# Four weight-sum columns beside the experts, expert inputs in two single buffers, and the norm's vector in the weights

## Chip, cores and metric

One core of a Trainium2 chip runs the whole program. The metric is the device time of one execution in microseconds, the median over the runs shown. TensorE multiplies, VectorE, ScalarE and GpSimd do the elementwise work, and DMAs are issued from the queue of SP (SyncE) and, for gathers, from GpSimd's.

## The reference, cut to what matters

Three layers follow each other: a windowed attention, a layer of eight experts of which each token uses two, and a gated layer behind a root-mean-square norm. The change touches the last two.

```python
x = attention(q, k, v)                         # 2304 tokens x 512
top2 of (x @ w_gate + noise * log1p(exp(x @ w_noise)))
out[t] = sum over the token's 2 experts e of weight * (relu(x[t] @ w1[e]) @ w2[e])   # 512 -> 1024 -> 512
x = out
rms = sqrt(mean(x * x) + 1e-6)
xn = x / rms * rms_g
g, val = xn @ w_gate, xn @ w_val               # 512 -> 1536 each
y = (g * sigmoid(g) * val) @ w_out             # 1536 -> 512
```

## The kernel before, in words

**Numbers as pairs.** Matrices are kept as two float16 parts, a rounded high part and the rest; a product takes three matmuls (high by high, low by high, high by low). ScalarE rounds (the high part), VectorE or GpSimd subtracts (the low part).

**Experts.** Each expert has room for 640 tokens (`CAP`). `row_steps` (lines 169 to 176) brings its rows from memory turned, by five DMA transposes, into the tile `xT`, of which there are two (experts take turns between two pools, `epool`). `expert_steps` (222) works in two pieces, 384 and 256 tokens: `first_steps` (178) makes hidden units in eight slices, with ScalarE's `hh` (194) and VectorE's `hl` (195) after each, then `second_steps` (206) multiplies them back. While expert e runs, VectorE and ScalarE also split the weights of expert e+1 (`weight_steps`, 98), and `m2_steps` (653) decodes and splits six slices of the gated layer's weights, scaled by a constant (662 to 666): the gate's in experts 1 and 2, the value's in 3 and 4, the output's in 5 and 6.

**The gated layer.** The first two tiles of 128 tokens go plainly: `gated` (858) makes gate and value products (line 880) for 12 chunks of 128 columns, and `projected` (903) multiplies with the output weights (914). The other 16 tiles go in four blocks of four through `quads` (1040), which needs 7 products in place of 8 per pair of chunks: sums of weight blocks times sums of token blocks (987). There are 12 such weight columns (6 chunk pairs by gate and value). For each, `weight_sums` (927) has VectorE make 8 sums (938), ScalarE round 4 (941) and GpSimd subtract 4 (944). Three columns are made beside the last expert (`SOON`), nine beside the first tiles of the gated layer. Their places are in `xpool`, `hpool` and `ppool`.

**Tokens of the gated layer.** `combine` (797) gathers each token's two expert rows by GpSimd (763), mixes them on VectorE (769, 770), normalizes by the root and the vector `rms_g` (`normal`, 745, with the vector broadcast to all partitions in `gb`), makes the token sums (823 to 826), splits them (837, 838) and turns them by DMA transposes into the one buffer `xq` (843). `combine_first` (773) does the first two tiles beside the last expert.

**Order.** Each engine runs its instructions in the order in which the program issues them, and the program writes this order by hand. `drive` (146) counts columns that TensorE has been given, and whenever a side task's due point (start, pace, task) is reached it issues that task's next step. One column count of 256 is one matmul of 256 columns. So `(0, SUMS, weight_sums(...))` with `SUMS` = 3200 issues one fifth of a weight column each 3,200 columns. The due points of the two main calls are at 1064 and 1094; those of the experts at 704 and 709. Pools that close return their room, and a tile put there waits for the last use of the tile that lay in its place.

Of the kernel before, what the change touches and what calls it, by code (L numbers as in the profile page):

```python
# [13 lines left out]
F32 = mybir.dt.float32  # L14
# [18 lines left out]
SOON, SUM0, SUMS = 3, 6000, 3200  # L33
# [8 lines left out]
def attention_moe_swiglu(  # L42
# [34 lines left out]
    hpool = ctx.enter_context(tc.tile_pool(name="hpool", bufs=1))  # L77
    early = ctx.enter_context(ExitStack())
# [16 lines left out]
    gb = consts.tile([P, DM], F32, name="gb")  # L95
# [73 lines left out]
    def row_steps(e, cs, taken=None):  # L169
        if cs.start == 0:  # L170
            xts[e] = epool[e % 2].tile([P, 2 * KC, CAP], F16, name="xT")
        for c in range(cs.start, cs.stop, P):
            ins = nc.sync.dma_start_transpose(xts[e][:, :, c:c + P], xrows[e * N + c:e * N + c + P, :])
            if taken is not None:
                taken.append(ins)
            yield

    def first_steps(hp_, w1h, w1l, xT, *pieces):
# [3 lines left out]
        for cs, f in itertools.product(pieces, range(FC)):  # L182
# [4 lines left out]
            for w1, xo in ((w1h, 0), (w1l, 0), (w1h, KC)):  # L187
                for c in range(KC):
                    nc.tensor.matmul(hp[:, :w], w1[:, c, f * P:(f + 1) * P], xT[:, xo + c, cs],  # L189
# [32 lines left out]
    def expert_steps(e, *pieces):  # L222
        w1h, w1l, w2h, w2l = wts[e]
        steps = first_steps(hpool, w1h, w1l, xts[e], *pieces)
# [14 lines left out]
    with ExitStack() as actx:  # L239
# [171 lines left out]
        def constants():  # L411
# [15 lines left out]
            nc.vector.tensor_scalar(gb, gb, SN, None, op0=OP.mult)  # L427
# [35 lines left out]
        def route(t0, nb):  # L463
# [49 lines left out]
            if t0 < 10:  # L513
# [9 lines left out]
        nc.sync.dma_start(gb, bass.AP(tensor=moe2_rms_g.tensor, offset=moe2_rms_g.offset,  # L523
                                      ap=[[0, P], [1, DM]]))
# [112 lines left out]
    m2w = ctx.enter_context(tc.tile_pool(name="m2w", bufs=1, side="right", reuse_waits="tile"))  # L637
    epool.append(late.enter_context(tc.tile_pool(name="epool1", bufs=1, side="right", reuse_waits="tile")))
    dec = late.enter_context(tc.tile_pool(name="dec", bufs=1, side="right", reuse_waits="tile"))
# [56 lines left out]

    coming = {}

    def ahead(e):
        if e < E:  # L700
# [5 lines left out]
          *((50000 + 9000 * i, 500, row_steps(1, cs)) for i, cs in enumerate(HALVES)),  # L706
          (40000, 4000, mix()), (70000, 5000, ahead(2)))
    for e in range(1, E - 1):
        drive(itertools.chain(*(expert_steps(e, cs) for cs in HALVES)),
              (2000, 3000, coming.pop(e + 1)), (106000, 5000, ahead(e + 2)),  # L710
              *((46000 + 17000 * i, 2000, row_steps(e + 1, cs)) for i, cs in enumerate(HALVES)),
              (48000, 2900, m2_steps([m2_part(i) for i in range(6 * (e - 1), 6 * e)])))

    early.close()
# [5 lines left out]
    HQ, QW, FH = QT // 2, QT // 2 * P, GC // 2  # L720
# [15 lines left out]
    def inverse(mp, vv, r):  # L736
# [36 lines left out]
    def combine_first(mp, xnT):  # L773
# [7 lines left out]
        for n in range(2 * FIRST + 3):  # L781
            for i in range(FIRST):
# [9 lines left out]
                elif j == 4:  # L792
                    inverse(mp, *rs[i])
                    turned(mp, x3s[i], rs[i][1], columns(xnT, i), nc.vector if i == FIRST - 1 else nc.gpsimd)
            yield

    def combine(mp, t0, xq):
# [19 lines left out]
        for j, (a, b) in enumerate(pairs):  # L817
            xa, xb = x3s[a], x3s[b]
            tt = mp.tile([P, 3, K2], F32, name="tt", bufs=1)
            normal(xa, r[:, a:a + 1])  # L820
            normal(xb, r[:, b:b + 1])
# [7 lines left out]
            for x in (xa, xb, tt[:, :2].rearrange("p k d -> p (k d)"), tt[:, 2]):  # L829
# [3 lines left out]
                else:  # L833
                    xn = mp.tile([P, DM], F16, name="xh", bufs=1)
# [11 lines left out]
    def normalize(mp, x3s, xnT):  # L846
# [5 lines left out]
        for i, x3 in enumerate(x3s):  # L852
            turned(mp, x3, r[:, i:i + 1], columns(xnT, i), nc.gpsimd)
# [68 lines left out]

    def weight_sums(mp, sw, chunks):
        for i, m in chunks:
            blocks = {}
            for a, k in itertools.product(range(2), range(2)):  # L930
                cs = slice((a * FH + i) * P, (a * FH + i + 1) * P)
# [235 lines left out]
```

## Time and profile before

| | us |
|---|---|
| median of 3 runs | 984.01 (982.09 to 984.03) |
| the profiled execution | 982.35 |
| its span, first to last instruction | 980.6 |
| TensorE busy | 950.8 (97%) |
| VectorE busy | 652.7 (67%) |
| ScalarE busy | 450.3 (46%) |
| GpSimd busy | 212.9 (22%) |

Attention runs until about 150 us, the experts until 564.6, the first two tiles of the gated layer until 623.3, and the four blocks of four tiles until the end. The clock granted to TensorE reads 9 (90% or more) in each of the page's 40 slices.

How to read it: PE is TensorE, PEld its weight loads, DVE VectorE, ACT ScalarE, POOL GpSimd, SPq the DMA queue of SP. "out<-in" names tiles, L938 a line of the kernel. In a bracket stands the idle time before an instruction and what ended it.

### The profile page before, as it was taken

What the parts mean: (1) busy time and instruction counts of PE and PEld (TensorE: products, weight loads), DVE (VectorE), ACT (ScalarE), POOL (GpSimd) and SP (SyncE); (2) the same over time, 40 slices, a digit from 0 to 9 for tenths busy, and PEclk for the clock granted to TensorE, in tenths of its full rate; (3) what the DMA queues carried; (4) which work ended last, traced back from release to release, by engine and by line L of the source; (5) the groups of instructions that cost most, each with busy time, mean ns of one, the idle gap of its engine ahead of it and who ended that gap; (6) DMA issues with size and microseconds to landing.
All of it is one profiled execution on the core that took longest, in us unless ns stands there. A gap on an engine that the chain in (4) does not pass through costs nothing.

```text
span 980.6 us, 18518 instructions
## 1 busy us (share of the span) xinstructions
PE 950.8 (97%) x7220; PEld 663.9 (68%) x7220; DVE 652.7 (67%) x1503; ACT 450.3 (46%) x920; POOL 212.9 (22%) x255
## 2 busy tenths in 40 slices
PE   7999999999999999999999997989999999999997
PEld 5998896656565555656565684678478658847864
DVE  6788767357576766666665579999458817944850
ACT  7999865254544444454533344434223422522320
POOL 5567644000000000000002364631601230130000
PEclk9999999999999999999999999999999999999999
DMA  7989667757584948495740242211431160122000
GB/s 235 309 246 241 176 184 200 208 158 208 174 234 151 250 137 220 156 230 168 210 112 14 76 114 44 60 54 33 105 69 33 22 151 1 34 64 57 1 13 35
DMA packets 145279, 127.12 MB, mean 130 GB/s; under 512 B 97696, under 2 KB 114848, under 8 KB 145184
## 3 DMA queue, kind: packets, MB, share of 16 engines
q1 hardware_dynamic: 139424, 106.99, 40.8%
q0 software_dynamic: 5760, 18.88, 5.8%
q8 instruction: 58, 0.95, 0.4%
q14 instruction: 37, 0.30, 0.1%
HBM read 76.81 MB, written 26.74 MB: 106 GB/s over the span
## 4 chain that ended last, share of the span: by engine, by line
PE 87%; DVE 7%; DMA 2%; ACT 1%; issue 1%; POOL 1%; SPq 1%; DVEq 0%; ACTq 0%; POOLq 0%
PE acc L210 21%; PE mm L189 21%; PE mm L987 21%; PE acc L914 11%; PE acc L363 6%; PE mm L349 4%; DVE sums L938 3%; PE mm L321 3%; DMA xq<-xg 1%; SPq L843 1%; DVE pgl L896 1%; PE rt L460 0%; PE mm L880 0%; DVE ya L770 0%; DMA yb<-ybuf,ysl 0%
## 5 line engine op out<-in xcount | busy, mean ns | idle before, releaser
L189 PE MATMUL mm<-xT,w1h 128*128 128x256 f16 (+2 forms) x1088 | 164.8, 291 | 0.0
L195 DVE SCALAR_TENSOR_TENSOR hl<-mm,hh 128x256 f16<-128x256 f32 (+2 forms) x136 | 63.8, 469 | 104.3 <-ACT hh L194 104.1
L189 PEld LDWEIGHTS <-w1h 128*128 128x128 f16 x1088 | 103.9, 98 | 37.8
L210 PE MATMUL acc<-w2h,hh 128*128 128x512 f16 x320 | 121.3, 379 | 0.0
L210 PE MATMUL acc<-w2l,hh 128*128 128x512 f16 x320 | 121.3, 379 | 0.0
L210 PE MATMUL acc<-w2h,hl 128*128 128x512 f16 x320 | 121.3, 379 | 0.0
L944 POOL TENSOR_TENSOR sw<-sums,sw 128x256 f16<-128x256 f32 x36 | 28.5, 810 | 387.9 <-ACT sw L941 387.9
L210 PEld LDWEIGHTS <-hh 128*128 128x128 f16 x640 | 62.6, 98 | 72.8
L987 PE MATMUL mm<-xq,sw 128*128 128x256 f16 x864 | 100.5, 273 | 1.6 <-DMA xq<-xg 1.5
L194 ACT ACTIVATE hh<-mm 128x256 f16<-128x256 f32 (+2 forms) x136 | 56.8, 418 | 85.8 <-PE mm L189 83.6
L987 PEld LDWEIGHTS <-sw 128*128 128x128 f16 x864 | 84.3, 98 | 12.3 <-issue 1.8
L189 PE MATMUL mm<-xT,w1l 128*128 128x256 f16 (+2 forms) x544 | 92.2, 291 | 0.0
L914 PE MATMUL acc<-oh__3213,pgl 128*128 128x512 f16 (+2 forms) x228 | 84.0, 371 | 2.9 <-DVE pgl L896 2.9
L914 PE MATMUL acc<-oh__3213,pgh 128*128 128x512 f16 (+2 forms) x228 | 83.9, 370 | 0.4 <-ACT pgh L894 0.4
L914 PE MATMUL acc<-ol__3214,pgh 128*128 128x512 f16 (+2 forms) x228 | 84.0, 371 | 0.0
L914 PEld LDWEIGHTS <-pgh 128*128 128x128 f16 x456 | 44.3, 99 | 49.9 <-issue 1.4
L363 PE MATMUL acc<-v,pf 128*128 128x96 f32 x544 | 72.6, 276 | 0.0
L363 PEld LDWEIGHTS acc<-v,pf 128*128 128x128 f32 x544 | 68.5, 197 | 0.0
L332 DVE CUSTOM_DVE_ANT_0 ss<-mm,bias 128x256 f32<-128x256 f32 (+1 forms) x144 | 54.1, 398 | 17.3 <-PE mm L321 11.5
L341 ACT ACTIVATE pr<-ss,nm 128x256 f32<-128x256 f32 (+1 forms) x144 | 63.2, 490 | 3.7 <-DVE nm L332 3.4
L189 PEld LDWEIGHTS <-w1l 128*128 128x128 f16 x544 | 52.1, 98 | 17.7
L232 ACT ACTIVATE ys<-acc 128x512 f32<-128x512 f32 x40 | 23.7, 593 | 77.3 <-PE acc L210 68.9
(190 smaller groups left out, 1721.0 us busy)
## 6 DMA issues: line engine op xcount, KB each, us to landing
st<-in_moe_w SPq DMA_DIRECT2D x64, 512.0 KB, 4.4
ybuf<-ys SPq DMA_DIRECT2D x40, 256.0 KB, 2.5
raw<-in_qkv SPq DMA_DIRECT2D x17, 512.0 KB, 5.3
st<-in_moe_w_gate SPq DMA_DIRECT2D x12, 512.0 KB, 5.0
st<-in_moe_w_val SPq DMA_DIRECT2D x12, 512.0 KB, 4.8
st<-in_moe_w_out SPq DMA_DIRECT2D x12, 512.0 KB, 5.2
v<-in_qkv SPq DMA_DIRECT2D x18, 279.0 KB, 5.3
out<-ys SPq DMA_DIRECT2D x17, 256.0 KB, 2.2
```

Source lines behind the costliest of these rows:

```text
L189: nc.tensor.matmul(hp[:, :w], w1[:, c, f * P:(f + 1) * P], xT[:, xo + c, cs], start=(n == 0), stop=(n == 3 * KC - 1))
L194: nc.scalar.activation(hh[:, f, hs], hp[:, :w], AF.Relu)
L195: nc.vector.scalar_tensor_tensor(hl[:, f, hs], hp[:, :w], 0.0, hh[:, f, hs], op0=OP.max, op1=OP.subtract)
L210: nc.tensor.matmul(yp, hx[:, f, i * P:(i + 1) * P], w2[:, f, :], start=(n == 0), stop=(n == 3 * FC - 1))
L321: nc.tensor.matmul(st[n + i]["sp"][:, j, c:c + w * P], qT[t][ds, a, h // 2, :], kT[ds, b, h // 2, sl:sl + w, :], start=(m == 0), stop=(m = ...
L332: nc.vector.tensor_tensor_reduce(out=d["ss"][:, j, c0:], in0=d["sp"][:, j, c0:], in1=bias[kind][:, heads(d["hp"])[j], c0:], scale=-1.0 / K ...
L341: nc.scalar.activation(d["pr"][:, j, c0:], d["ss"][:, j, c0:], AF.Exp, scale=-1.0, bias=d["nm"][:, j:j + 1])
L349: nc.tensor.transpose(pt[:, j, kk, :], d["pr"][:, j, kk * P:(kk + 1) * P], ident)
L363: nc.tensor.matmul(xps[t, hp // 2][:, h % 4, :VN], ph[:, j, kk, :], v32[t - 1 + kk][:, h * DV:h * DV + VN], start=(kk == k0), stop=(kk == 1))
L914: nc.tensor.matmul(op[:, ds], px[:, f, cs], w[:, f, ds], start=(k == 0), stop=(k == 3 * GC - 1))
L938: nc.vector.tensor_tensor(out=o, in0=x, in1=y, op=op)
L987: nc.tensor.matmul(pp, w(a, pa, c), xq[:, 4 * b + 2 * pb + c, :], start=(n == 0), stop=(n == 5))
```

## The change

- Four of the nine weight columns that were made beside the gated layer are made beside experts 3 to 6, one in each (30,000 columns into the expert, a step each 5,500), in a new pool `spool`. Three are still made beside the last expert, at a pace of 3,000 columns per step in place of 6,000, and five beside the gated layer, at 4,400 in place of 3,200. They use fewer temporary buffers: one in `spool` and one in `mp`, by turns.
- The expert inputs lie in two tiles, `xA` (384 tokens) and `xB` (256), one of each, in place of two `xT`. The second piece of an expert's rows is now brought at that expert's own start (due at 1,000 columns), no longer in the expert before.
- The vector of the norm is multiplied into gate and value weights where they are split: `gain` holds it by rows of the weights (with the constants), and `m2_part` hands a column of it as scale. `normal` goes; tokens are scaled by the root alone, on ScalarE (`combine`, `turned`). `SN` moves into the last step of `inverse`.
- Buffers of the gated layer (`gt`, `vt`, `p1`, `tt`, `xh`) move to a pool `mp2` on the other side; some sums' places move into `xA` and `xB`; the pool `dec` closes earlier.

```diff
-SOON, SUM0, SUMS = 3, 6000, 3200
+SOON, SUM0, SUMS = 3, 3000, 4400
...
     def row_steps(e, cs, taken=None):
-        if cs.start == 0:
-            xts[e] = epool[e % 2].tile([P, 2 * KC, CAP], F16, name="xT")
+        first = cs.start < GW
+        if cs.start in (0, GW):
+            xts[e, first] = xpiece.tile([P, 2 * KC, GW if first else CAP - GW], F16, name="xA" if first else "xB")
...
-        nc.sync.dma_start(gb, bass.AP(tensor=moe2_rms_g.tensor, offset=moe2_rms_g.offset,
-                                      ap=[[0, P], [1, DM]]))
+        nc.sync.dma_start(gain[:, 0], moe2_rms_g.rearrange("(c p) -> p c", p=P))
...
-            src, sc = ((moe2_w_gate, SWG), (moe2_w_val, SWV))[m]
-            return (src[c * P:(c + 1) * P, n0:n0 + DM], sc, *(x[:, c, n0:n0 + DM] for x in gw[2 * m:2 * m + 2]))
+            src = (moe2_w_gate, moe2_w_val)[m]
+            return (src[c * P:(c + 1) * P, n0:n0 + DM], gain[:, m, c:c + 1], *(x[:, c, n0:n0 + DM] for x in gw[2 * m:2 * m + 2]))
...
+    chunks = list(itertools.product(range(FH), range(2)))
+    EARLIER = {3: [(0, 0)], 4: [(1, 0)], 5: [(0, 1)], 6: [(1, 1)]}
+    BESIDE = len(EARLIER)
+    sw = {at: [spool.tile([P, 2, 2, 2, P], F16, name=f"sw{at[0]}{at[1]}_{j}") for j in range(2)] for at in chunks[:BESIDE]}
...
-          *((50000 + 9000 * i, 500, row_steps(1, cs)) for i, cs in enumerate(HALVES)),
+          (50000, 500, row_steps(1, HALVES[0])),
           (40000, 4000, mix()), (70000, 5000, ahead(2)))
     for e in range(1, E - 1):
         drive(itertools.chain(*(expert_steps(e, cs) for cs in HALVES)),
               (2000, 3000, coming.pop(e + 1)), (106000, 5000, ahead(e + 2)),
-              *((46000 + 17000 * i, 2000, row_steps(e + 1, cs)) for i, cs in enumerate(HALVES)),
+              (1000, 2000, row_steps(e, HALVES[1])), (46000, 2000, row_steps(e + 1, HALVES[0])),
+              (30000, 5500, weight_sums([spool], sw, EARLIER.get(e, ()))),
               (48000, 2900, m2_steps([m2_part(i) for i in range(6 * (e - 1), 6 * e)])))
...
-        nc.vector.tensor_tensor(out=r, in0=r, in1=u, op=OP.mult)
-    def normal(x3, r):
-        nc.vector.scalar_tensor_tensor(x3, x3, r, gb, op0=OP.mult, op1=OP.mult)
-    def turned(mp, x3, r, xnT, lo):
-        normal(x3, r)
+        nc.vector.scalar_tensor_tensor(r, r, SN, u, op0=OP.mult, op1=OP.mult)
+    def turned(mp, x3, r, xnT):
         xn = mp.tile([P, 2 * DM], F16, name="xg", bufs=3)
-        nc.vector.tensor_copy(xn[:, :DM], x3)
-        lo.tensor_tensor(out=xn[:, DM:], in0=x3, in1=xn[:, :DM], op=OP.subtract)
+        nc.scalar.activation(xn[:, :DM], x3, AF.Copy, scale=r)
+        nc.vector.scalar_tensor_tensor(xn[:, DM:], x3, r, xn[:, :DM], op0=OP.mult, op1=OP.subtract)
...
-            normal(xa, r[:, a:a + 1])
-            normal(xb, r[:, b:b + 1])
+            for i in (a, b):
+                nc.scalar.activation(x3s[i], x3s[i], AF.Copy, scale=r[:, i:i + 1])
...
-        drive(itertools.chain(*(expert_steps(E - 1, cs) for cs in HALVES)), (0, SUM0, weight_sums(mp, sw, chunks[:SOON])),
+        drive(itertools.chain(*(expert_steps(E - 1, cs) for cs in HALVES)), (1000, 2000, row_steps(E - 1, HALVES[1])),
+              (0, SUM0, weight_sums([spool, mp], sw, chunks[BESIDE:BESIDE + SOON])),
...
-        drive(blocks(), (0, SUMS, weight_sums(mp, sw, chunks[SOON:])),
+        drive(blocks(), (0, SUMS, weight_sums([spool, mp], sw, chunks[BESIDE + SOON:])),
```

## Rows read from the trace of the kernel before

**Rows 1.** The page, busy time of each engine, its share of the span, instructions

```profile
PE 950.8 (97%) x7220; PEld 663.9 (68%) x7220; DVE 652.7 (67%) x1503; ACT 450.3 (46%) x920; POOL 212.9 (22%) x255
```

**Rows 2.** Waits of TensorE: waited for, us in total, times, longest

```profile
PE mm L880 <- DVE gt L892: 3.1, 1, 3.1
PE acc L914 <- DVE pgl L896: 2.9, 1, 2.9
PE mm L987 <- ACT p L1008: 2.6, 2, 2.0
```

**Rows 3.** Windows: stretch, us, busy PE, PEld, DVE, ACT, POOL; PEclk; DMA

```profile
564.64:602.50 37.86, 33.48 (x313) 29.35 (x312) 30.85 (x66) 19.87 (x51) 20.62 (x25) 0.95 0.25 74
602.50:623.30 20.80, 17.56 (x74) 7.29 (x72) 19.87 (x30) 7.65 (x19) 14.56 (x15) 0.92 0.46 90
623.30:683.53 60.23, 56.07 (x506) 49.19 (x505) 56.13 (x92) 25.58 (x48) 19.21 (x22) 1.00 0.15 44
888.60:943.64 55.04, 55.04 (x506) 49.28 (x504) 41.10 (x57) 16.71 (x24) 0.00 (x0) 1.00 0.02 6
```

**Rows 4.** The chain that ended last, in order of time: start us, us

```profile
857.54 31.08 PE acc L914 x144
888.62 55.02 PE mm L987 x504
```

**Rows 5.** The same windows view, one slice of 4 us behind a stall

```profile
592.00:596.00 4.00, 4.00 (x26) 3.04 (x24) 2.83 (x10) 3.42 (x10) 1.30 (x2) 0.62 0.00 0
```

**Rows 6.** Timeline of VectorE, first block: start us, us, instruction, idle before

```profile
578.88 1.10 DVE L770 SCALAR_TENSOR_TENSOR ya<-yb,cw,ya 128x512 f32<-128x512 f32 x1 [1.08 <-DMA yb<-ybuf,ysl]
...
585.33 0.41 DVE L892 TENSOR_TENSOR vt<-vt,mm 128x256 f32<-128x256 f32 x1
...
591.20 0.41 DVE L892 TENSOR_TENSOR gt<-gt,mm 128x256 f32<-128x256 f32 x1
...
611.96 0.41 DVE L896 TENSOR_TENSOR pgl<-gt,pgh 128x256 f16<-128x256 f32 x1
```

**Rows 7.** Timeline of ScalarE, first block and first four-tile block

```profile
601.40 0.61 ACT L837 ACTIVATE xg<-ya 128x512 f16<-128x512 f32 x1
...
644.41 0.42 ACT L941 ACTIVATE sw<-sums 128x256 f16<-128x256 f32 x1 [2.93 <-DVE sums L938]
```

**Rows 8.** VectorE after the experts: line 938 alone (windows), and line 746 (groups)

```profile
564.64:646.00 81.36, 38.89 (x68) 0.96 0.25 64
...
L746 DVE SCALAR_TENSOR_TENSOR ya<-ya,r,gb 128x512 f32<-128x512 f32 x4 | 2.8, 741 | 0.0
```

**Rows 9.** Timeline of GpSimd, first block: requests for gathered rows

```profile
575.16 0.95 POOL L763 DMA_INDIRECT yb<-ybuf,ysl  x1 [0.30 <-issue]
...
585.76 1.14 POOL L763 DMA_INDIRECT yb<-ybuf,ysl  x1 [0.30 <-DVE vt L892]
```

**Rows 10.** Expert 3: windows view, and the last low half in VectorE's timeline

```profile
304.90:356.90 52.00, 52.00 (x315) 30.53 (x313) 35.19 (x62) 25.23 (x49) 0.00 (x0) 1.00 0.67 192
...
348.85 0.42 DVE L195 SCALAR_TENSOR_TENSOR hl<-mm,hh 128x256 f16<-128x256 f32 x1
```

**Rows 11.** Timeline of SP's queue in expert 3

```profile
305.99 12.77 SPq L109 DMA_DIRECT2D st<-in_moe_w  x5
318.81 3.71 SPq L173 DMA_TRANSPOSE xT<-xrows  x2
```

**Rows 12.** Timeline of SP's queue, first block

```profile
603.38 5.50 SPq L843 DMA_TRANSPOSE xq<-xg  x3
...
620.70 1.23 SPq L843 DMA_TRANSPOSE xq<-xh  x1
```

**Rows 13.** Instructions on the sums' tile: ns min/median/max

```profile
L938 DVE TENSOR_TENSOR sums<-vh__3211,sums x6: 413/774/891, 531.2 to 642.7; 128x256 f32<-128x256 f16 x6
...
L944 POOL TENSOR_TENSOR sw<-sums,sw x36: 659/811/1747, 519.6 to 644.9; 128x256 f16<-128x256 f32 x36
```

**Rows 14.** Timeline of SP's queue at the start

```profile
7.33 3.17 SPq L523 DMA_DIRECT2D gb<-in_moe_rms_g  x1
```

More of the change, by code (lines that the diff above doesn't have):

```diff
@@ L93, in attention_moe_swiglu @@
     tops = consts.tile([P, NT, 2], F32, name="tops")
-    gb = consts.tile([P, DM], F32, name="gb")
+    gain = consts.tile([P, 2, KC], F32, name="gain")
     wts = {}
@@ L223, in expert_steps, with x @@
         w1h, w1l, w2h, w2l = wts[e]
-        steps = first_steps(hpool, w1h, w1l, xts[e], *pieces)
+        def x(c, cs):
+            first = cs.start < GW
+            at = 0 if first else GW
+            return xts[e, first][:, c, cs.start - at:cs.stop - at]
+        steps = first_steps(hpool, w1h, w1l, x, *pieces)
         hh, hl = next(steps)
@@ L426, in constants @@
                            allow_small_or_imprecise_dtypes=True)
-            nc.vector.tensor_scalar(gb, gb, SN, None, op0=OP.mult)
+            nc.vector.tensor_scalar(gain[:, 1], gain[:, 0], SWV, None, op0=OP.mult)
+            nc.vector.tensor_scalar(gain[:, 0], gain[:, 0], SWG, None, op0=OP.mult)
             for e in range(E):
@@ L695, in mix, with weight_sums, add, hi @@
         nc.vector.tensor_tensor(out=cw[:, :, 1], in0=cd, in1=cw[:, :, 0], op=OP.mult)
+    def weight_sums(pools, sw, chunks):
+        pools = itertools.cycle(pools)
+        for i, m in chunks:
+            blocks = {}
+            for a, k in itertools.product(range(2), range(2)):
+                cs = slice((a * FH + i) * P, (a * FH + i + 1) * P)
+                blocks[a, k] = [w[:, 2 * k:2 * k + 2, cs] for w in gw[2 * m:2 * m + 2]]
+            here = [[sw[i, m][k // 2][:, k % 2, part] for part in range(2)] for k in range(4)]
+            temps = next(pools).tile([P, 4, 2, P], F32, name="sums", bufs=1)
+            s, u, v, x = (temps[:, j] for j in range(4))
+            def add(o, x, y, op):
+                nc.vector.tensor_tensor(out=o, in0=x, in1=y, op=op)
+            def hi(k, x):
+                nc.scalar.activation(here[k][0], x, AF.Copy)
+            def lo(k, x):
+                nc.gpsimd.tensor_tensor(out=here[k][1], in0=x, in1=here[k][0], op=OP.subtract)
+            add(u, *blocks[0, 0], OP.add)
+            add(v, *blocks[1, 0], OP.add)
+            yield
+            add(s, v, blocks[1, 1][0], OP.add)
+            add(s, s, blocks[1, 1][1], OP.add)
+            yield
+            hi(0, s)
+            add(v, u, v, OP.subtract)
+            add(u, s, u, OP.subtract)
+            yield
+            hi(2, v)
+            lo(0, s)
+            add(x, blocks[0, 1][0], u, OP.subtract)
+            add(x, blocks[0, 1][1], x, OP.add)
+            yield
+            hi(1, u)
+            hi(3, x)
+            lo(2, v)
+            yield
+            lo(1, u)
+            lo(3, x)
+    FH = GC // 2
+    chunks = list(itertools.product(range(FH), range(2)))
+    EARLIER = {3: [(0, 0)], 4: [(1, 0)], 5: [(0, 1)], 6: [(1, 1)]}
+    BESIDE = len(EARLIER)
+    sw = {at: [spool.tile([P, 2, 2, 2, P], F16, name=f"sw{at[0]}{at[1]}_{j}") for j in range(2)] for at in chunks[:BESIDE]}
     coming = {}
@@ L719, in attention_moe_swiglu @@
     FIRST, QT = 2, 4
[L720 removed]
+    HQ, QW = QT // 2, QT // 2 * P
     def square(mp, x3, sq):
@@ L793, in combine_first, with combine @@
                     inverse(mp, *rs[i])
-                    turned(mp, x3s[i], rs[i][1], columns(xnT, i), nc.vector if i == FIRST - 1 else nc.gpsimd)
+                    turned(mp, x3s[i], rs[i][1], columns(xnT, i))
             yield
-    def combine(mp, t0, xq):
+    def combine(mp, mp2, t0, xq):
         ys, x3s = {}, {}
@@ L852, in normalize @@
         for i, x3 in enumerate(x3s):
-            turned(mp, x3, r[:, i:i + 1], columns(xnT, i), nc.gpsimd)
+            turned(mp, x3, r[:, i:i + 1], columns(xnT, i))
     def products(ppool):
@@ L1123, in attention_moe_swiglu @@
                 normalize(mp, [mixed(t + i, *gather(mp, t + i, True)) for i in range(G)], xnT)
-                for _ in itertools.chain(gated(mp, ph, pl, t, G, xnT), projected(ph, pl, t, G, range(GC))):
+                for _ in itertools.chain(gated(mp2, ph, pl, t, G, xnT), projected(ph, pl, t, G, range(GC))):
                     pass
```

83 lines of the change are left out of this document (25 added, 58 removed).

## The prediction, made before the changed kernel was built

> **What bounds the kernel now.** I began with the page's busy times: TensorE works 950.8 of 980.6 us [rows 1], so a change that leaves every matmul in place can win back only TensorE's idle time and what it runs at the lower clock. The list of waits by engine puts the idle time after 564 us: TensorE waits there for VectorE, or for a ScalarE that itself waits for VectorE [rows 2]. The busy time by stretch gives it by block: 37.86 - 33.48 = 4.4 us idle in the first block's gate and value products, 20.80 - 17.56 = 3.2 us in its projection, 60.23 - 56.07 = 4.2 us in the first block of four tiles; the last block of four tiles has none [rows 3].
>
> How long should these blocks take? The chain of waits shows the same work undisturbed: 504 products of 256 columns in 55.02 us (0.109 us each) and 144 projections of 512 columns in 31.08 us [rows 4]. The first block has 12 x 24 = 288 products, 31.4 us instead of 37.9, a loss of 6.4; its 72 projections need 15.5 instead of 20.8, a loss of 5.3; the first block of four loses 60.2 - 55.0 = 5.2. Together **16.9 us**. That is 5 more than the idle time because the granted clock falls after a stall: 0.62 in the slice right behind the 3.1 us wait (1.00 is 2.4 GHz, so part of the slice ran at 1.2) [rows 5]; the means of the first two stretches are 0.95 and 0.92 [rows 3].
>
> Why does VectorE come late? In the timeline the release of the value bank (line 892) runs at 585.33 and the next at 591.20, 5.9 us apart where a chunk of products takes 24 x 0.109 = 2.6 us; the next-to-last low half (line 896) runs at 611.96, 9.5 us after TensorE has ended the gate products at 602.5 [rows 3, 6]. Between these stand weight sums (line 938) and the normalization (line 746). In the four-tile block ScalarE stands in its queue before a rounding of sums until VectorE has made them, 2.93 us, and only then copies out the bank that TensorE wants [rows 7].
>
> **The change part by part.**
>
> *Sums moved.* From 564.64 to 646 us VectorE spends 38.89 us on 68 sums, 0.572 us each [rows 8]; a column takes 8, so 4.6 us. Nine columns are made there now, five afterwards: 28 of the 68 instructions go, 16.0 us. The new pace (one step each 4,400 columns instead of 3,200) puts 17 steps instead of 24 ahead of the end of the gate products, and all 25 (5 columns of 5 steps, 110,000 columns) before the first block of four (110,592). So that block, which lost 5.2 us, has no sums left in it and looks like the last block [rows 3].
>
> *Norm's vector folded.* Four multiplications of 0.741 us leave VectorE per block of four tiles, 3.0 us [rows 8], and become ScalarE copies like the 0.61 us one of the same size [rows 7], 2.4 us on an engine busy 19.87 of 37.86 us [rows 3]. In the first two tiles two casts go to ScalarE as well and one subtraction comes from GpSimd to VectorE; this ends slightly sooner, and its cover is the rest of the last expert.
>
> VectorE thus loses 19 of the 30.85 + 19.87 + 56.13 = 106.9 us that it works in the three stretches [rows 3], which last 118.9 us and would last 102 without the loss. That leaves 87.9 of 102, 86%: demand falls below supply, so the queue no longer grows. (The last block does with 41.10 of 55.04.)
>
> *What stays in the gate products.* Two of the four gathered row pairs are mixed between two bank releases, whatever is done to the sums. A row was on hand 2.8 us after the end of GpSimd's 0.95 us instruction that asked for it, and VectorE waited 1.08 us for one [rows 6, 9]. The fourth pair's request runs at 585.76 [rows 9], behind weight subtractions of some 0.8 us each [rows 13]; 585.76 + 1.14 + 2.8 = 589.7, and the release came at 591.20. With seven steps fewer ahead, up to five subtractions, it comes some 3 us sooner, so the release at 588. TensorE wants that bank 8.5 chunks of 2.62 us behind 564.64, at 587: **1.2 us remain** (0 to 4.4).
>
> *What is late next.* The four-tile block needs its turned inputs. Now the first transposes start at 603.38, behind the gate products, and the last is issued by 621.9, 18.5 us later [rows 12]; TensorE needs 15.5 us for the projection and uses the last piece 6 products of 0.65 us later, at 19.5. The second pair's come late now because VectorE does. Without that the first pair's buffers set them: issue 5.5 + 1.3 us [rows 12], landing 2.8 as for a gathered row (an estimate), rounding and subtraction some 2, issue and landing of the last 4, with the 0.9 us at the start 16.5 in all. It fits by 3 us; I take 0.5 (0 to 4).
>
> *Beside the experts.* Experts 3 to 6 get 8 sums, 4 ScalarE copies and 4 GpSimd subtractions each. On VectorE that is 3.4 us by the 0.42 us of an undisturbed sum, 4.6 by the mean, and up to 6.2 if each took 0.774 [rows 8, 13]. Expert 3 leaves VectorE 52.0 - 35.19 = 16.8 us idle with TensorE never waiting [rows 10]. The sums stand from column 30,000 to 57,500, mostly in the first second-product, where TensorE asks nothing of VectorE. The next due point is the last low half before the second piece's second product: done at 349.3 [rows 10], wanted, by the rates above [rows 4] from the expert's start, at 304.9 + 15.7 + 15.5 + 10.5 + 22 x 0.216 = 351.4. I take 0 (0 to 2.5 us per expert).
>
> Sums on VectorE beside GpSimd were stretched, from 0.413 to 0.774 us in the median of one form, GpSimd's subtraction from 0.659 to 1.747 [rows 13]. The Trainium skill, "SBUF — State Buffer", section "Who interferes with whom", says that a VectorE instruction with two SBUF inputs and a GpSimd one that reads SBUF exclude each other for the whole instruction. This speaks against the change, since GpSimd is idle beside the experts now. By that rule four subtractions of 0.66 us would hold VectorE 2.6 us more per expert (an estimate); that lies inside the idle time above and the sum stays, but rival 3 below, priced from rows alone, would cost 35 us instead of 24.
>
> *Halved, single-buffered inputs.* The transposes are as many, moved. The first half's (three) are issued where they were, but the queue of SP runs ahead: in expert 3 it issued two at 318.81 [rows 11], and the one buffer is only free when TensorE has read it, at 304.9 + 96 x 1.5 x 0.109 = 320.6. So SP stands 1.8 us with the next weight loads behind it, for work that ends well inside the expert. The second half's two now come at the start of their own expert, ahead of the loads that block SP for 12.77 us [rows 11], 28 us before they are needed. Cost 0 for both; if that cover went, 1.2 us of SP each.
>
> *The rest.* The vector arrives in 512 short pieces instead of a broadcast that held SP 3.17 us [rows 14]; VectorE scales it with its constants long before the weights need it, and the loads behind it on SP are for later tiles. A gain of 3 us or a hold of as much at that place, 0 on TensorE. Weights scaled by a column instead of a constant are not in the trace; line 746 has such a scale at the same size, 0.741 us [rows 8], so even against a free constant it is 6 x 0.741 = 4.4 us of an expert's 16.8 idle. Gate buffers now lie where the last expert's weights were, whose last read is before their first write. Last expert: three columns at twice the pace put 2.5 of them, 8.5 to 11.5 us, into its first product of 15.7 us beside eight low halves; VectorE may end that 1 us behind, and then has 15.5 us in which TensorE asks for nothing. All 0.
>
> **Sum.** 16.9 - 1.2 - 0.5 = 15.2 us back. The profiled execution took 982.35 us (span 980.6 and 1.75 around it): 967.2. It lies 1.7 us under the median of 984.0, which gives 968.8 by that scale; I take **968.5**.
>
> **Rivals.**
> 1. *The turned inputs become the bound.* If the chain of transposes keeps its 18.5 us, it ends 0.9 + 18.5 + 2.8 = 22.2 us behind the gate products and TensorE waits 2.7 us, up to 4 with the pieces used before the last, and the clock falls again for 2: 3 to 6 us given back, 970 to 975 on the median's scale. For it: three buffers and one queue. Against: the second pair's lateness is VectorE's. 0.13.
> 2. *The gathered rows hold the first block.* Its 6.4 us stay, clock included: 982.35 - 10.5 + 0.5 = 972.4, 974 by the median. For it: the 1.08 us wait. Against: that row is at most 1.1 of the 5.9 us between releases. 0.10.
> 3. *Slower: VectorE in the experts.* If the stretched sums push the second piece's low halves past their 2.1 us of margin, TensorE stalls in four experts. From 3.8 us each (stall and fallen clock) the gain is gone; with 6.2 us of delay passed on in full it is 6.2 - 2.1 and 2 of clock, 6.1 each: 968.5 + 24 = 993; with 4.0 each, 984.5. Against: 16.8 us of idle time per expert. 0.05.
> 4. *No effect:* the stalls have another cause than VectorE's load, and 984 stays. The timeline speaks against it. 0.03.
>
> **How the numbers follow.** The forecast has 0.69 and spans 965 (all of the 16.9) to 970. A measurement of this kernel tells about 0.2% from no change, 2 us. Forecast and rivals 1 and 2 are faster: 0.92; same 0.03; slower 0.05. The range runs from 964.5 (everything back and a little of the later waits) to 977, over rivals 1 and 2 with their clock.
>
> **What would show it.** Right: no TensorE waits on lines of gate products, projection and first four-tile block but one near 1 us; a granted clock of 1.0 throughout; 40 sums on VectorE after the experts; busy time of TensorE unchanged but for the clock; expert 3 still 52.0 us. Wrong: a wait of the first four-tile block for transposes (rival 1), a gap at a value bank behind a gathered row (2), an expert longer than 52 us (3).

## The result, and the profile after

The changed kernel takes **972.21 us** (median of 4 runs, 972.07 to 974.03) against 984.02 of the kernel before (4 runs, 982.09 to 984.64): ratio **0.989** (0.987 to 0.991, a 95% interval as behind every ratio here), 11.8 us less. Faster, as forecast, though by only 1.1%, and inside the range of 964.5 to 977, but 3.7 us above the forecast of 968.5. The profiled execution took 972.07 us with a span of 970.4, against 982.35 and 980.6: 10.2 us to be found in the traces.

The lines have moved: 943 is the old 880 (gate and value products), 955 and 959 the old 892 and 896, 977 and 1005 the old 914 and 987; 725, 728 and 731 are the sums, their rounding and their subtraction (938, 941, 944), 832 and 833 the mixing (769, 770), 826 the gather (763), 906 the transposes (843), 200 the low half in the experts (195). Line 884 is the new scaling by the root.

Windows of the kernel after; columns as in [rows 3]. The first stretch is expert 3 [rows 10], the others are the gate products, the projection and the first block of four tiles [rows 3]:

```profile
303.87:355.87 52.00, 52.00 (x314) 30.55 (x313) 40.18 (x70) 26.79 (x53) 4.19 (x4) 1.00 0.64 190
563.61:600.12 36.51, 32.13 (x313) 28.47 (x312) 25.03 (x56) 19.65 (x49) 15.70 (x20) 1.00 0.23 69
600.12:615.97 15.85, 15.74 (x74) 6.89 (x72) 15.06 (x23) 7.66 (x18) 11.13 (x11) 1.00 0.50 88
615.97:672.26 56.29, 55.20 (x506) 49.23 (x505) 47.51 (x74) 23.22 (x39) 12.78 (x15) 1.00 0.21 56
```

Read against [rows 3] the first number of each line gives the result by place. The forecast below is the prediction's own sum, split by stretch (gate products 6.4 - 1.2, projection 5.3, four tiles 5.2 - 0.5).

| | before | after | won | forecast |
|---|---|---|---|---|
| attention, to the first expert's second product | 164.40 | 163.37 | 1.03 | 0 |
| the eight experts from there on | 400.24 | 400.24 | 0.00 | 0 |
| gate products of the first block | 37.86 | 36.51 | 1.35 | 5.2 |
| projection of the first block | 20.80 | 15.85 | 4.95 | 5.3 |
| first block of four tiles | 60.23 | 56.29 | 3.94 | 4.7 |
| the rest | 297.1 | 298.1 | -1.07 | 0 |
| sum | 980.6 | 970.4 | 10.2 | 15.2 |

The 1.03 us of attention I count as chance: the change touches little there (the norm's vector, the place of the first expert's rows), and from 120 to 140 us the granted clock was 0.91 in the profile before and 1.00 in this one. So nearly all that is missing lies in **the gate products**. Their clock is 1.00 now (0.95 before), but 36.51 - 32.13 = 4.38 us of idle time are left, as much as before. TensorE's timeline shows the four waits in this stretch, and the one at the start of the four-tile block (in a bracket the idle time before the instruction and what ended it):

```profile
584.16 0.60 PE L943 MATMUL mm<-xq,vh__3218 128*128 128x256 f16 x4 [0.68 <-DVE vt L955]
...
588.81 0.60 PE L943 MATMUL mm<-xq,vh__3218 128*128 128x256 f16 x4 [1.88 <-DVE gt L955]
...
594.78 0.60 PE L943 MATMUL mm<-xq,vh__3218 128*128 128x256 f16 x4 [0.56 <-DVE gt L955]
...
598.82 0.60 PE L943 MATMUL mm<-xq,vh__3218 128*128 128x256 f16 x4 [1.26 <-DVE vt L955]
...
618.54 1.70 PE L1005 MATMUL mm<-xq,sw 128*128 128x256 f16 x14 [1.09 <-DMA xq<-xg]
```

VectorE's timeline, first its two waits for gathered rows, then all that stands between two of these bank releases, at 583.70 and 588.34:

```profile
577.10 0.48 DVE L832 TENSOR_SCALAR ya<-ya,cw 128x512 f32<-128x512 f32 x1 [1.54 <-DMA ya<-ybuf,ysl]
578.64 0.81 DVE L833 SCALAR_TENSOR_TENSOR ya<-yb,cw,ya 128x512 f32<-128x512 f32 x1 [1.05 <-DMA yb<-ybuf,ysl]
...
583.70 0.41 DVE L955 TENSOR_TENSOR vt<-vt,mm 128x256 f32<-128x256 f32 x1
584.03 0.56 DVE L832 TENSOR_SCALAR ya<-ya,cw 128x512 f32<-128x512 f32 x1
584.62 2.29 DVE L833 SCALAR_TENSOR_TENSOR ya<-yb,cw,ya 128x512 f32<-128x512 f32 x1
586.83 0.47 DVE L832 TENSOR_SCALAR ya<-ya,cw 128x512 f32<-128x512 f32 x1
587.34 0.75 DVE L833 SCALAR_TENSOR_TENSOR ya<-yb,cw,ya 128x512 f32<-128x512 f32 x1
588.01 0.42 DVE L959 TENSOR_TENSOR pgl<-vt,pgh 128x256 f16<-128x256 f32 x1
588.34 0.42 DVE L955 TENSOR_TENSOR gt<-gt,mm 128x256 f32<-128x256 f32 x1
```

and GpSimd's at the same time:

```profile
582.48 0.95 POOL L826 DMA_INDIRECT yb<-ybuf,ysl  x1 [0.30 <-DVE sums L725]
583.45 0.85 POOL L731 TENSOR_TENSOR xA<-sums,xA 128x256 f16<-128x256 f32 x1
584.26 0.84 POOL L731 TENSOR_TENSOR xB<-sums,xB 128x256 f16<-128x256 f32 x1
585.07 0.66 POOL L731 TENSOR_TENSOR xA<-sums,xA 128x256 f16<-128x256 f32 x1
585.70 0.66 POOL L731 TENSOR_TENSOR xB<-sums,xB 128x256 f16<-128x256 f32 x1
```

There is no weight sum between the two releases. The mixings of two token tiles stand there, where TensorE wants a bank each 2.6 us, and one of the two took 2.29 us instead of 0.75. GpSimd's timeline shows why just then: four subtractions that had queued behind eight gather requests (573.63 to 583.43) run back to back. Those 1.54 us too many are most of the second wait (1.88 us). The first wait has another cause, since its release (583.70) ran before the stretched mixing began: VectorE came late to it after it had itself waited 1.54 and 1.05 us for the first gathered rows. The fourth pair's request, which the prediction looked at, ran 3.3 us sooner than before [rows 9], or 2.3 us sooner counted from the end of the experts (some 3 forecast); its data were no longer what was waited for.

Before the third and the fourth release VectorE waits for ScalarE. The five short steps of the root stand in VectorE's queue ahead of the release at 594.32, and the rounding of products ahead of the one at 598.35:

```profile
592.71 0.18 DVE L804 RECIPROCAL r<-r 128x4 f32<-128x4 f32 x1 [0.83 <-ACT r L800]
...
598.01 0.43 DVE L959 TENSOR_TENSOR pgl<-gt,pgh 128x256 f16<-128x256 f32 x1 [2.50 <-ACT pgh L957]
```

ScalarE's timeline has two loads of an activation table and the two scalings in these places:

```profile
591.18 1.28 ACT L800 ACT_TABLE_LOAD   x1
...
594.47 1.28 ACT L948 ACT_TABLE_LOAD   x1 [1.18 <-DVE pgl L959]
...
596.35 1.32 ACT L884 ACTIVATE ya<-ya,r 128x512 f32<-128x512 f32 x2
```

The Trainium skill, "SBUF — State Buffer", section "Who interferes with whom", says that a VectorE instruction with two SBUF inputs contends with a GpSimd instruction that reads SBUF. These rows agree: the mixing reads two tiles and was stretched by 1.54 us beside the three subtractions from 584.26 on (0.84, 0.66, 0.66 us).

Beside the experts the sums cost TensorE nothing. In expert 3 VectorE's eight sums took 4.25 us, and the last low half of the second piece came 45.5 us after the expert's start (44.4 in [rows 10]) where the prediction had worked out that it is wanted at 46.5:

```profile
319.15 0.75 DVE L725 TENSOR_TENSOR sums<-gh,gl 128x256 f32<-128x256 f16 x2
...
321.10 0.42 DVE L725 TENSOR_TENSOR sums<-sums,gh 128x256 f32<-128x256 f32 x1
...
321.56 0.42 DVE L725 TENSOR_TENSOR sums<-sums,gl 128x256 f32<-128x256 f32 x1
...
323.10 1.35 DVE L725 TENSOR_TENSOR sums<-sums 128x256 f32<-128x256 f32 x2
...
326.06 0.89 DVE L725 TENSOR_TENSOR sums<-gh,sums 128x256 f32<-128x256 f16 x1
...
326.98 0.42 DVE L725 TENSOR_TENSOR sums<-gl,sums 128x256 f32<-128x256 f16 x1
...
348.98 0.42 DVE L200 SCALAR_TENSOR_TENSOR hl<-mm,hh 128x256 f16<-128x256 f32 x1
```

### The profile page after: what moved, and what is told of

It is laid out like the page before. It is cut to its first block, busy times and chain, and to the rows that moved or that the text cites. A ratio compares the mean times of both kernels' runs of the same rounds, so it can differ in the third digit from the quotient of the medians.

```text
span 970.4 us, 18521 instructions
## 1 busy us (share of the span) xinstructions
PE 944.6 (97%) x7220; PEld 660.5 (68%) x7220; DVE 642.2 (66%) x1485; ACT 463.0 (48%) x938; POOL 210.5 (22%) x254
## 4 chain that ended last, share of the span: by engine, by line
PE 86%; DVE 4%; issue 3%; DMA 3%; POOL 1%; ACT 1%; SPq 1%; POOLq 0%; DVEq 0%; ACTq 0%
PE mm L1005 22%; PE acc L215 20%; PE mm L194 20%; PE acc L977 11%; PE acc L373 6%; PE mm L359 3%; PE mm L331 3%; DMA xq<-xg 1%; SPq L906 1%; DVE sums L725 1%; DMA raw<-in_qkv 1%; PE rt L471 0%; DVE pgl L959 0%; DVE ya L833 0%; DMA yb<-ybuf,ysl 0%
## 5 line engine op out<-in xcount | busy, mean ns | idle before, releaser
L731 POOL TENSOR_TENSOR sw<-sums,sw 128x256 f16<-128x256 f32 x28 | 25.8, 927 | 343.8 <-ACT sw L728 343.4
L194 PE MATMUL mm<-xA,w1h 128*128 128x384 f16 (+2 forms) x576 | 97.1, 308 | 0.0
L1005 PE MATMUL mm<-xq,sw 128*128 128x256 f16 x672 | 77.9, 273 | 3.1 <-DMA xq<-xg 3.1
L1005 PEld LDWEIGHTS <-sw 128*128 128x128 f16 x672 | 65.6, 98 | 11.3 <-issue 2.3
L194 PE MATMUL mm<-xB,w1h 128*128 128x256 f16 x512 | 67.7, 273 | 0.0
L1026 ACT ACTIVATE p<-mm 128x256 f32<-128x256 f32 x48 | 18.3, 382 | 88.9 <-PE mm L1005 88.7
```

Of the source, the lines that this page charges most:

```text
L194: nc.tensor.matmul(hp[:, :w], w1[:, c, f * P:(f + 1) * P], xT(xo + c, cs), start=(n == 0), stop=(n == 3 * KC - 1))
L731: nc.gpsimd.tensor_tensor(out=here[k][1], in0=x, in1=here[k][0], op=OP.subtract)
L1005: nc.tensor.matmul(pp, w(a, pa, c), xq[:, 4 * b + 2 * pb + c, :], start=(n == 0), stop=(n == 5))
```

## The experiments

Ten runs on three other chips: e1 to e4 on the second chip, r_after and e5 to e7 on the third, r_e7 and e8 on the fourth. There the kernel before takes 995.4, 998.1 and 996.6 us. In the traces of these runs attention alone is some 12 to 16 us longer (the first expert's second product starts at 175.1 to 179.6 us, at 163.4 above); the experts without added work are not. So ratios to the kernel before on the same chip are compared, and lengths of stretches. All edits are made to the changed kernel.

**e1: the scaling by the root back on VectorE.** The last of the four waits ends behind a ScalarE that had loaded a table (594.47, 1.28 us) and done two scalings (596.35, 1.32 us) before the rounding that VectorE waited for.

```diff
-                nc.scalar.activation(x3s[i], x3s[i], AF.Copy, scale=r[:, i:i + 1])
+                nc.vector.tensor_scalar(x3s[i], x3s[i], r[:, i:i + 1], None, op0=OP.mult)
```

> The changed kernel, with the four-tile blocks' scaling by the root back on VectorE (one multiplication of some 0.48 us per tile in place of ScalarE's 0.66 us copy). In the changed kernel TensorE waits four times in the gate products: 0.68, 1.88, 0.56 and 1.26 us. Theory A (the waits come from gathered rows that are mixed between two bank releases, and from GpSimd's subtractions next to them): the first two waits stay near 2.6 us, the last two too, and the time is 972.2 within 1 us. Theory B (the scaling and the table loads stand in ScalarE's queue ahead of the rounding that VectorE waits for): the last two waits, 1.8 us, shrink below 0.8 and the first two stay; time 971.

Measured: 982.89 us, ratio 0.987 (0.985 to 0.989), gate products 37.49, projection 16.07, four tiles 56.24. Inconclusive by itself: on this chip the gate products had three waits of TensorE for nothing that the profile shows and a clock of 0.91, and none for VectorE. So neither theory is decided: e6 moves the scaling too, but on top of e4, where the two waits in question are gone already.

**e2: the moved sums back beside the gated layer**, with fold, buffers and pools left as changed.

```diff
-SOON, SUM0, SUMS = 3, 3000, 4400
+SOON, SUM0, SUMS = 3, 6000, 3200
...
-              (30000, 5500, weight_sums([spool], sw, EARLIER.get(e, ()))),
...
-              (0, SUM0, weight_sums([spool, mp], sw, chunks[BESIDE:BESIDE + SOON])),
+              (0, SUM0, weight_sums([spool, mp], sw, chunks[:SOON])),
...
-        drive(blocks(), (0, SUMS, weight_sums([spool, mp], sw, chunks[BESIDE + SOON:])),
+        drive(blocks(), (0, SUMS, weight_sums([spool, mp], sw, chunks[SOON:])),
```

> The changed kernel with no sums beside experts 3 to 6: all nine columns are made beside the gated layer again at the old paces, everything else (halved inputs, folded vector, pools) as changed. If the moved sums carry the gain: 979 to 982, with TensorE waits in the projection and the first four-tile block back (3.2 and 4.2 us idle) and a granted clock below 1.0 there. If the folded vector and the new places carry it: 972 to 975.

Measured: 994.55 us, ratio **0.9995** (0.998 to 1.001): the whole gain is gone. The three stretches of e2:

```profile
575.33:613.89 38.56, 33.65 (x314) 29.35 (x312) 28.68 (x64) 21.03 (x53) 20.21 (x25) 0.96 0.22 67
613.89:631.89 18.00, 16.07 (x74) 6.80 (x72) 17.11 (x26) 8.10 (x19) 13.14 (x13) 1.00 0.49 94
631.89:693.61 61.72, 57.34 (x505) 50.01 (x504) 57.62 (x93) 26.31 (x50) 20.86 (x24) 0.97 0.16 46
```

Each is longer than its counterpart after, and the waits of [rows 2] are back (3.09 us for a release by VectorE; 1.54 in the projection; 2.30 and 2.00 for ScalarE's `p`). The expected 979 to 982 stand on the first chip's scale, where they would leave 2 to 5 us of the gain; nothing is left of it. So the moved sums carry the gain, together with their paces, which this edit also sets back. Fold, single buffers and other pools give nothing that can be measured by themselves; they make the room. The other half of the test, the kernel before with the moved sums alone, was not run.

**e3: two columns beside each of experts 3 to 6** (the same column twice, the second result unused), at twice the pace.

```diff
-              (30000, 5500, weight_sums([spool], sw, EARLIER.get(e, ()))),
+              (30000, 2750, weight_sums([spool], sw, 2 * EARLIER.get(e, []))),
```

> The changed kernel with every sum beside experts 3 to 6 made twice (the second time over the first, at twice the pace), which doubles the cost put there: 8 sums, 4 roundings and 4 subtractions more per expert. If VectorE's idle time covers it, experts still last 52.0 us and the time stays at 972.2. If the margin of the last low half (349.4 done, 350.4 wanted in the changed kernel, 1.0 us) is what counts, experts 3 to 6 grow by 1 to 3 us each and the time is 976 to 984.

Measured: 1001.41 us, ratio 1.006 (1.004 to 1.008). The windows of expert 2, without sums, and of experts 3 and 6, with two columns:

```profile
264.60:316.58 51.98, 51.98 (x314) 30.54 (x312) 35.54 (x62) 25.44 (x49) 0.00 (x0) 1.00 0.67 193
316.58:372.86 56.28, 52.30 (x314) 30.50 (x313) 44.23 (x78) 27.90 (x57) 7.52 (x8) 1.00 0.60 173
485.53:541.86 56.33, 53.80 (x313) 31.40 (x312) 44.43 (x80) 27.20 (x57) 7.53 (x8) 0.97 0.59 171
```

The row of TensorE's waits that holds the loss (columns as in [rows 2]):

```profile
PE mm L194 <- DVE hl L200: 13.1, 6, 3.0
```

Experts 3 to 6 take 56.3, 56.8, 55.8 and 56.3 us instead of 52.0: 17.3 us in all, of which 13.1 are waits for low halves; 1 to 3 us an expert had been expected. VectorE still idles 12 us in such an expert. Twice the sums bring the mechanism of rival 3, at about the price that it named (4.0 to 6.1 us an expert); one column stays below the point from which it decides, two do not.

The gate products of e3 are those of the changed kernel, on the chip of e4, and take 36.49 us there: TensorE waits 0.89, 0.56 and 1.26 us for VectorE, the last two as on the first chip, and 1.48 us for nothing that the profile shows.

**e4: gathering and mixing spread.** The first block of four tiles is prepared from 13,728 columns on instead of 21,728, and one token tile's gather and mixing each 6,000 columns instead of each 4,000, so that one mixing falls on a chunk.

```diff
-AHEAD, PACE = (13, 9), (4000, 8000)
+AHEAD, PACE = (20, 9), (3000, 8000)
...
             yield
+            if t0 == FIRST:
+                yield
```

> The changed kernel with the first four-tile block's gathers asked for earlier and 6,000 columns apart in place of 4,000, so that a row has two steps of 2.6 us to land and only one tile is mixed between two bank releases; the later steps (root, scaling, splitting) stay near where they were. Theory A: VectorE's waits for gathered rows (1.54 and 1.05 us) and TensorE's first two waits (2.6 us) go, time 969.5 to 970.5. Theory B: the waits of the gate products only move behind the root and stay near 4 us, time 972.

Measured: 980.23 us, ratio 0.984 (0.982 to 0.987). Gate products 32.34 us (window in two parts: 2.68 before the first bank release, 29.66 behind it), projection 16.92, four tiles 55.89. The window behind the first release:

```profile
578.35:608.01 29.66, 29.14 (x267) 25.83 (x265) 25.09 (x55) 14.77 (x41) 14.98 (x18) 1.00 0.25 72
```

TensorE's timeline has one wait in it:

```profile
601.21 0.60 PE L945 MATMUL mm<-xq,vh__3218 128*128 128x256 f16 x4 [0.43 <-DVE vt L957]
```

VectorE does as much work as after (25.09 us) in 4.2 us less (32.34 against 36.51, and against 36.49 in e3 on the same chip): what stalled TensorE was the order. But the edit changes more of the order than the mixings. No row is waited for any more; and since each round of gathering and mixing now takes two steps, the root comes 6,000 columns later: its five steps begin 3.0 us ahead of the end of the gate products (7.4 in the kernel after), and the first scalings run 0.6 us behind that end (3.8 ahead of it). So e4 removes the four waits (but for the 0.43 us) without saying which of these moves removed which. One mixing was stretched to 2.29 us here too (at 594.88), and no wait followed, because the second mixing came only after the next release. The projection pays 1.1 us, with two waits of 0.38 and 0.39 for the last products' halves. TensorE's first two waits went, as theory A has it, and the last two too, which neither theory had; the times of both stand on the first chip's scale.

**r_after: the changed kernel again, on the third chip.**

> The changed kernel again, unchanged, so that the next three have it on the same chip: ratio to the kernel before 0.987 to 0.990, the first gate products 36.5 us from the last expert's end to the projection, with 4.4 us of waits for VectorE, where that stretch shows no waits of other kinds.

Measured: 986.14 us, ratio 0.987 (0.985 to 0.990), as on the first chip. Gate products 37.97, projection 15.84, four tiles 56.25. The gate products have waits of another kind than on the first chip (2.8 us for nothing that the profile shows, 0.2 for VectorE; rows in the last section), so the 4.4 us of waits for VectorE could not be seen again here; e3 shows three of the four.

**e5: GpSimd's subtractions of the last five columns on VectorE.**

```diff
-                nc.gpsimd.tensor_tensor(out=here[k][1], in0=x, in1=here[k][0], op=OP.subtract)
+                on = nc.vector if (i, m) in chunks_late else nc.gpsimd
+                on.tensor_tensor(out=here[k][1], in0=x, in1=here[k][0], op=OP.subtract)
```

> The changed kernel with the low halves of the last five columns' sums made by VectorE in place of GpSimd (20 subtractions of 0.42 us or more added to VectorE, GpSimd left with gathers and tokens). If GpSimd's subtractions are what stretches VectorE (one mixing took 2.29 us beside four of them, 0.75 us alone), VectorE's sums fall to 0.42 us each and the second wait (1.88 us) below 0.8, gate products 35 us or less. If it is VectorE's load that counts, 8.4 us more make the stretch to the end of the first four-tile block 2 to 6 us longer than the changed kernel's 108.6.

Measured: 984.30 us, ratio 0.986 (0.983 to 0.989). Gate products 34.30, 0.52 of it a wait for turned inputs at their start, projection 16.42, four tiles 56.04: 106.8 us together, not more than 108.6, so VectorE's load does not decide. The first two waits are gone and every mixing takes 0.75 us; the last two remain (0.55 and 1.26). With its subtractions gone GpSimd also asks for the first rows sooner (4.0 us behind the start of the gate products, 10.0 in the kernel after), and VectorE no longer waits for them. So the first two waits come from what GpSimd's queue did to VectorE, by late rows and by the stretched mixing, and the last two from something else.

**e6: e4 and e1 together.**

> Gathers 6,000 columns apart and the scaling by the root on VectorE, together. With the gathers apart alone the gate products took 32.3 us, the projection 16.9, the first four-tile block 55.9. Theory A (only the spread of the mixing counted): the same 105.2 us within 0.5. Theory B (ScalarE's queue holds VectorE by 2.6 us before the token sums): the projection's two waits of 0.4 us go and it takes 15.6 to 16.0.

Measured: 983.59 us, ratio 0.986 (0.983 to 0.989). Gate products 32.32 (32.34 in e4), projection 17.39 (16.92), with a wait of 1.09 where e4 had 0.38, four tiles 56.21: 105.9 us together, 0.2 above theory A's bound. With the gathers apart, where the scaling stands changes nothing in the gate products, and the theory that ScalarE's scaling holds the projection falls: that got longer, not shorter.

**e7: e4, and the later blocks prepared 8,000 columns earlier** (`AHEAD` = (20, 10)).

> Gathers 6,000 columns apart, and in the later blocks every step of a block's tokens issued 8,000 columns sooner, so that the second pair's transposes stand ahead of an output store in SP's queue. If the order in SP's queue is what delays the turned inputs of the second and third four-tile blocks, TensorE's two waits there (0.9 and 0.7 us at the second product, 2.2 us with the tiles' edges) go and the ratio is 0.982 against 0.984 for the gathers alone; if the transposes themselves are too slow, no change.

Measured: 980.47 us, ratio **0.982** (0.980 to 0.985), against 0.987 of the changed kernel on the same chip. The waits for turned inputs in the later blocks are gone. (In the kernel after, SP's queue stands 7.55 us at output stores at 689.18, ahead of the second pair's transposes at 696.82. The edit makes every step of the preparation sooner, so whether the place behind the store or the date of the steps was at fault is not separated.) The list of waits of the kernel after has three, one in the first block of four and two later:

```profile
PE mm L1005 <- DMA xq<-xg: 3.1, 3, 1.1
```

In e7 (its second run, r_e7) one is left, in the first block of four:

```profile
PE mm L1007 <- DMA xq<-xg: 0.6, 1, 0.6
```

**r_e7 and e8: e7 again, and e7 with e5.**

> The version with gathers 6,000 columns apart and later blocks one step earlier, again, to confirm its gain: ratio 0.980 to 0.985 to the kernel before.

> The same with the low halves of the last five columns' sums on VectorE. If the subtractions beside GpSimd cost VectorE more than doing them itself, the projection's waits (0.4 and 0.4 us) and the first four-tile block's (0.6 us) go and the ratio is 0.001 below the version without; if VectorE's load decides, the projection takes 17.5 us or more and the ratio is the same or above.

Measured: 980.41 us, ratio 0.984 (0.982 to 0.986), and 979.27, ratio 0.982 (0.980 to 0.984). The stretches of r_e7 are 32.33, 16.92 and 56.81, the last 0.9 us longer than in e4, which takes back part of what the later blocks gain; those of e8:

```profile
578.33:610.92 32.59, 31.76 (x314) 28.54 (x313) 23.89 (x65) 17.04 (x44) 6.09 (x6) 1.00 0.26 74
610.92:627.84 16.92, 16.14 (x74) 6.80 (x72) 14.16 (x27) 10.42 (x24) 10.12 (x10) 1.00 0.51 98
627.84:682.86 55.02, 55.02 (x505) 49.28 (x504) 49.02 (x83) 23.22 (x40) 7.18 (x7) 1.00 0.18 52
```

In e8 the first block of four tiles takes 55.02 us, as long as the undisturbed one [rows 3], and TensorE waits nowhere in a later block. The projection's two waits stay, 0.39 and 0.39, against the expectation. The two versions' intervals overlap; both beat the kernel before (0.982 to 0.984). On the third chip, which ran both, e7 takes 0.9943 of the changed kernel's time (980.47 / 986.14), and each run of e7 is shorter than each of r_after. The intervals of e4 and e7 overlap, so what the earlier later blocks add is shown by the waits, not by the time. Neither version was run on the first chip.

## Why the prediction was right, and where it was not

*What bounds the kernel.* Right. But for attention's 1.03 us, by chance, time came back only where TensorE had waited for VectorE; e2 shows that the sums' place decides over all of it that can be measured.

*Sums moved.* Right. 40 sums stand after the experts (36 from 563.61 us on, 4 just ahead). The projection takes 15.85 us (forecast 15.5), the four-tile block has lost its wait for ScalarE behind the sums [rows 7], though the last four sums still run in it (the prediction had none there).

*What stays in the gate products.* **The step that failed: "1.2 us remain".** The idle time stayed at 4.4 us, the upper end of the step's own bounds (0 to 4.4); only the fallen clock was won, 32.13 us busy against 33.48. The step followed the fourth pair's row to one release, which it put 23.4 us behind the experts' end and TensorE's wish for the bank 22.4; measured are 24.7 and 23.3. The row was no longer what held it. The step itself says that two mixings stand between two releases, but it priced only the row's arrival and not the mixings, of which one was stretched to 2.29 us; and it took three other releases as on time because VectorE's load over the three stretches was below 100% (86%). In the gate products the load was 25.03 of 36.51, 69%, with four waits. That it is the order and not the load e4 shows, which keeps the work: 32.34 us, near the forecast's 32.6 (37.86 - 5.2), with the mixings spread and the root moved to the end. e5 splits the cause: GpSimd's subtractions, through rows asked for late and the stretched mixing, make the first two waits. For the last two the rows point to ScalarE, whose table loads and scalings VectorE waits for ahead of the releases, but no run shows it by itself: e1 could not tell, and e6 moves the scaling only where e4 has removed these waits. The sign named for a right forecast, no waits in these places but one near 1 us, did not come; the granted clock and the 52.0 us of the experts did.

Rival 2, in which this block's 6.4 us stay, gave 974 (972.4 on the scale of the profiled execution, which took 972.07); the time lies between it and the forecast, nearer to the rival. Its mechanism is there in part, as VectorE's waits of 1.54 and 1.05 us for gathered rows; it is not the whole, as the stretched mixing and the root show.

*What is late next.* The turned inputs were waited for 1.09 us, forecast 0.5. The transposes were issued from 602.23 to 617.74 us, 15.5 us where rival 1 had 18.5, so its 2.7 us and more did not come, though its sign did, a wait for transposes. Two things were off. The piece that was waited for was wanted 1.5 us into the block, sooner than the last piece on which the prediction went (3.9 us); and the chain was slower than its 16.5 us behind the gate products, since this piece, not yet the last, landed 18.4 us behind them. The mechanism was right, its term 0.6 us too small. In the later blocks the same wait grew from 1.5 us to 2.0; the prediction named no cost there, since it stopped at the first four-tile block. e7 shows that it goes when the preparation is issued 8,000 columns sooner. The other 0.6 of the 1.07 us lost in the rest has no cause shown here.

*Beside the experts.* 0 forecast, 0.00 measured. The margin of 2.1 us worked out for the last low half shrank to 1.0, by 1.16 us of delay where up to 6.2 had been allowed for. e3 shows that the margin was real and small. GpSimd's four subtractions were stretched (4.19 us in expert 3 instead of 2.6), but the eight sums took 4.25 us, less than the 4.6 that the mean gave.

*Single-buffered inputs.* 0, right: each expert still takes 52.00 us. SP's queue in expert 3, where the second half's transposes stand at the start and the next first half's wait for the tile to be free:

```profile
304.92 3.38 SPq L178 DMA_TRANSPOSE xB<-xrows  x2
308.40 9.32 SPq L111 DMA_DIRECT2D st<-in_moe_w  x5
319.50 2.85 SPq L178 DMA_TRANSPOSE xA<-xrows  x2
```

*The fold.* 0 for TensorE, right. A split with a column as scale takes 0.748 us, with the constant 0.688: 0.4 us of VectorE per expert, where the bound against a free constant had been 4.4. A pair of scalings takes 1.32 us on ScalarE (2 x 0.61 by the row). The vector's load in short pieces held SP 3.14 us, the broadcast 3.17 [rows 14]: neither the gain nor the loss of 3 us.

*The sum.* 15.2 us forecast; 1.35 + 4.95 + 3.94 came back there, the rest gave 1.07 away, and attention gave 1.03 in return, which is luck and no part of the forecast. On the medians 11.8 us, since the profiled execution before lay 1.7 us under its median.

## What to carry to other kernels

Load below 100% says that a queue does not grow; it does not say that each release in it is on time. Where one engine both frees banks and prepares the next block, read its timeline between two releases and count what stands there, its own waits for rows and for other engines too, against the interval in which the bank is wanted. Cover is used up in steps: one more task of 4 us was free in each of four experts, the next one cost 4 us in each, so work out the margin of the last due instruction and not the idle time of the engine (12 us were left idle).

## What was not expected of the hardware

- **A mixing of 0.75 us took 2.29 us**, beside GpSimd subtractions that ran back to back; the 1.54 us too many are more than any one of them took (0.84 at most). With the subtractions on VectorE (e5) every mixing took 0.75.
- **TensorE waited without a visible cause** in r_after, e1 and e3, in the gate products, and the clock fell in r_after and e1 (0.91 over the stretch). r_after, TensorE's timeline, and the windows of the slices behind:

```profile
595.92 0.27 PE L943 MATMUL mm<-xq,vh__3218 128*128 128x256 f16 x1 [0.47 <-issue]
597.34 0.27 PE L943 MATMUL mm<-xq,vh__3218 128*128 128x256 f16 x1 [1.15 <-issue]
598.75 0.38 PE L943 MATMUL mm<-xq,vh__3218 128*128 128x256 f16 x1 [1.14 <-issue]
```

```profile
597.00:598.50 1.50, 0.27 (x1) 0.00 (x0) 0.40 (x1) 0.00 (x0) 1.48 (x3) 0.77 0.65 194
598.50:600.00 1.50, 1.25 (x7) 0.90 (x8) 1.12 (x3) 1.03 (x4) 0.32 (x2) 0.50 0.35 128
...
602.00:606.00 4.00, 4.00 (x27) 3.08 (x26) 3.90 (x12) 1.45 (x5) 0.00 (x0) 0.67 0.00 0
```

  Between 595.4 and 598.5 TensorE was busy 0.59 of 3.1 us, and the granted clock went from 1.00 to 0.50 (1.2 GHz). What it waited for stays open. In r_after the eight gather requests run back to back just before and beside it (587.24 to 597.04), with the DMA engines busy at 0.65 to 0.72; in e2 and in e4 to e8, where the requests are spread or run sooner, such waits do not occur in the gate products. That the gathers cause them is not shown: the kernel after has the same requests on the first chip, and no such wait.
- **The clock held through short waits.** In the kernel after it reads 1.00 across waits of 0.68 to 1.88 us; behind those of 3.1 us it had read 0.62 [rows 5], and 0.57 in e2.
- **Chips differ more than the change is worth**: 984.0 us for the kernel before on one, 995.4 to 998.1 on three others, where it was not profiled. For the changed kernel the traces of the first and the third chip have 13.5 us of the difference (970.4 and 984.8 us of span) before the first expert's second product, 1.5 in the gate products, and none in the experts (52.0 us each). Waits without a visible cause are part of it: in the first expert's first product every run on the other chips has 1.4 to 4.3 us of them, the two profiles on the first chip none.
